# Two middle batches of a and b by Strassen block products: seven for eight, after the last attention

## The chip, the cores and the metric

One Trainium2 chip, one core. The metric is the device time of one launch in microseconds (us). The kernel before has a median of 718.08 us in three runs (717.61 to 720.74).

## The reference

Four batches of 12-head attention with a sigmoid in place of softmax, then a gated product, then a soft mixture of eight experts, all in float32:

```python
attn = sigmoid(q @ k.T / sqrt(64) - log(448))        # 4 batches, 12 heads, 448 x 64
x = (attn @ v) as 1792 x 768                          # 448 rows per batch
g = (x @ w_a) * (x @ w_b)                             # 1792 x 1536
y = g @ w_out                                         # 1792 x 768
logits = y @ phi                                      # 1792 x 32 slots
d = softmax of logits over the 1792 tokens; c = softmax over the 32 slots
slot_in = d.T @ y; h = relu(slot_in @ w1[e]); slot_out = h @ w2[e]   # 8 experts, 768 x 1024
out = c @ slot_out
```

## The kernel before, in words

Matrices lie with their inner dimension on the 128 partitions. `x` of a batch is six transposed tiles of 128 x 448 (one for each pair of heads); `w_a` and `w_b` are cut into 12 chunks of 128 columns (`fc`), each chunk 128 x 768 (six blocks of 128). Every float32 factor is split in two reduced-precision parts, high and low, and three of the four partial products are summed: high by high, low by high, high by low.

**Attention** (`att`, L211). A pair of heads (24 in all, six per batch) goes through these steps: `emit_TK` and `emit_TQ` transpose k and q on TensorE and split them on VectorE; `emit_S` (L171) makes the scores of one chunk of keys and the sigmoid on ScalarE; `emit_PV` (L190) multiplies by v; `emit_x` (L200) splits the result into the tiles `xh` (ScalarE) and `xl` (VectorE). The pairs of batch 0 run first, with nothing else on TensorE but some preparation.

**The gated product** (`ab`, L488). For each chunk `fc` of a batch it makes a, then b: 18 matmuls of 128 x 448 each (three partial products by six blocks, L502). ScalarE copies a out of PSUM (L509), VectorE multiplies b into it (L512); the result is a tile `gT`. So a batch has 12 x 2 x 18 = 432 matmuls of L502, the kernel 1728. Six of them are a step: after each step the generator yields, and the main loop (L754) lets the attention of the next batch go on by as much as it is due (`att_to`), so the attention of batches 1, 2 and 3 lies between the steps of `ab(0)`, `ab(1)` and `ab(2)`. `ab(3)` has no attention beside it. In `ab(0)` the weights are also converted (`beats`, L385) and stored in DRAM (`ab32`); later batches read them back (`load_w`) and split them again (`split`, L420): high part on VectorE (L425), low part on GpSimd (L426).

**Fill.** After every step of `ab` that wasn't preceded by a transposition, `fill_step` runs one step of the first generator in the list `fill`. `group(b, gi)` (L453) takes four `gT`: part of the logits (L461), 16 transpositions (L476), evacuated by ScalarE and VectorE in turn into `gk_01` or `gk_2`. `LG(b)` (L585) turns a batch's logits into exponentials (`logits`, L537), transposes them (`tokens`, L569) and multiplies them by the batch's three `gk` tiles (`dg`, L576, 64 matmuls at L582). A batch has three groups and one LG; those of batch 3 end after `ab(3)`. Both take PSUM banks from `ms()`, of which there are two up to batch 3; transpositions of k and q take theirs from the same two.

**The last batch and the experts.** With `ab(3)` the pool `e1` opens, and `pump` (L684, L757) starts to load the experts' weights into 17 slots of 1 MB, one pump for each three steps. All loads and stores go out by SyncE's queue (SP) in the order in which they are written, and a load that must wait for its buffer holds all later ones back. After `ab(3)` the experts' weights, 50 MB, are streamed and used (L809, L835).

Of the kernel before, what the change touches and what calls it, by code (L numbers as in the profile page):

```python
# [9 lines left out]
F32 = mybir.dt.float32  # L10
# [23 lines left out]
def body(ctx, tc, q, k, v, w_a, w_b, w_out, phi, w1, w2, out):  # L34
# [5 lines left out]
    ps_ctx, ab_ctx, x0_ctx, cv_ctx, ma_ctx, at_ctx = (ctx.enter_context(ExitStack()) for _ in range(6))  # L40
# [7 lines left out]
    more_a = {}  # L48
# [32 lines left out]
    ls_d = x0p.tile([128, 2 * S + 2 * C * NS], F32, name="ls_d")  # L81
# [7 lines left out]
    clog32 = drp.tile([T, C, B, NS], F32, name="clog32")  # L89

# [80 lines left out]
    def emit_S(g, chunks):  # L171

        (kh, kl), (qh, ql) = stk[g]["k"], stk[g]["q"]
        for c in chunks:
            ab = g < NP and c == 2
# [23 lines left out]

    def emit_x(g):  # L200
# [3 lines left out]
        xh = (x0p, x1p)[b % 2].tile([128, S], F32R, tag=f"xh{kk}", name=f"xh{kk}")  # L204
        xl = (x0p, x1p)[b % 2].tile([128, S], F32R, tag=f"xl{kk}", name=f"xl{kk}")
        act.activation(xh, pv, AF.Copy)  # L206
        dve.tensor_tensor(xl, pv, xh.bitcast(F32), op=ALU.subtract)  # L207
        xt[g] = (xh, xl)
        load_qkv(g + 3, "v")

    def att():  # L211
# [3 lines left out]
        for g in range(B * NP + 1):  # L215
            more = g < B * NP
            first = ((0, 1) if g == 0 else (0,) if g < NP else ()) if more else ()
# [6 lines left out]
            if g > 2 * NP:  # L224

                if g % 2 == 0:
                    emit_PV(g - 2, (0, 1, 2, 3))
                    emit_PV(g - 1, (0, 1, 2, 3))
                    emit_x(g - 2)
                    emit_x(g - 1)  # L230
                    yield 6400
            elif g:
                if g < NP:
# [5 lines left out]
            elif more:  # L239
                emit_TK(g + 1)  # L240
                yield 430
            if more and g >= NP:
# [6 lines left out]
            elif more:  # L249
# [135 lines left out]
    def beats():  # L385
        stage0(0)
        for x in range(len(jobs) + LAG + 2):
            if x < len(jobs):
                stage1(x)
            elif x == len(jobs):  # L390
                flush()
                for i in range(4):
                    load_w(2 * KF + i)
# [35 lines left out]
    def prep(n):  # L429
# [5 lines left out]
        elif 2 * n < LAST:  # L435
            for i in range(2):
                split(n, w_raw.pop(2 * n + i), dve.tensor_copy)
                for _ in range(3 if n == KF else 1):
# [465 lines left out]
```

## Time and profile before

| | us |
|---|---|
| median of three runs | 718.08 |
| profiled execution | 719.5 |
| its span, first to last instruction | 717.4 |
| TensorE busy in the span | 680.7 |

The profile is of one execution. Engines: PE is TensorE, PEld its weight loads, DVE is VectorE, ACT ScalarE, POOL GpSimd, SP SyncE. L502 is line 502 of the kernel. "PEclk" and "clock" are the share of its 2.4 GHz that TensorE was granted. Matmuls overlap, so a matmul's own duration is longer than the distance from one to the next. The chain of waits is the work that ended last, followed back to the start: what stands on it sets the time.

### The profile page before, as it was taken

Reading aid. Unit: us, or ns where it says so; the run is one execution under the profiler, and the core shown is the slowest. Engines: PE = TensorE matmul, PEld = TensorE weight load, DVE = VectorE, ACT = ScalarE, POOL = GpSimd, SP = SyncE. Lnnn points to the kernel's source line nnn. Section 1 sums busy time; section 2 is a strip of 40 time slices with the busy share of each in tenths; the row PEclk is TensorE's granted clock in tenths of the full one; section 3 lists DMA queues with packets and bytes.
Section 4 is the critical chain, followed back from the end, with each engine's and each line's share of the span. In section 5 each row is a group of like instructions: output and inputs, shape, how many; then the busy total and the mean of one; then the engine's idle time right before and its main releaser. Section 6 shows DMA issues by size and latency. Waiting matters only on the chain.

```text
span 717.4 us, 10851 instructions
## 1 busy us (share of the span) xinstructions
PE 680.7 (95%) x4231; PEld 489.8 (68%) x4231; DVE 303.2 (42%) x451; ACT 272.6 (38%) x469; POOL 246.3 (34%) x151
## 2 busy tenths in 40 slices
PE   7999999999999999999999999999999999998684
PEld 4547876776777687687776886878888896433132
DVE  4767899889843323234234232322322232300022
ACT  4987787877734324233143242331201011100021
POOL 0244677666653233242332322432444441100000
PEclk9999999999999999999999999999999999999898
DMA  8999999898762332423422322310788956999998
GB/s 208 243 283 228 293 314 295 262 301 276 227 202 54 104 100 75 122 71 87 143 61 92 104 66 61 103 50 1 264 276 325 359 209 217 364 415 417 410 353 273
DMA packets 107474, 148.99 MB, mean 208 GB/s; under 512 B 51360, under 2 KB 84384, under 8 KB 104352
## 3 DMA queue, kind: packets, MB, share of 16 engines
q1 hardware_dynamic: 107424, 148.31, 63.8%
q8 instruction: 33, 0.54, 0.3%
q14 instruction: 17, 0.14, 0.1%
HBM read 128.46 MB, written 19.83 MB: 207 GB/s over the span
## 4 chain that ended last, share of the span: by engine, by line
PE 84%; DMA 9%; DVE 2%; ACT 2%; issue 1%; POOL 0%; SPq 0%; ACTq 0%; POOLq 0%
PE ab L502 49%; PE sc L195 11%; PE sc L181 9%; DMA e<-in_moe_w 8%; PE ms L148 3%; PE ms L476 2%; PE ms L461 1%; DMA gkp<-in_moe_w 1%; PE ms L582 1%; DVE gk L323 1%; PE ms L366 1%; PE ms L353 1%; PE sc L872 1%; PE ab L835 1%; PE sc L789 1%
## 5 line engine op out<-in xcount | busy, mean ns | idle before, releaser
L426 POOL TENSOR_TENSOR wl<-wr_all,wh 128x768 fp32r<-128x768 f32 x50 | 92.0, 1841 | 207.2 <-DVE wh L425 98.3
L502 PE MATMUL ab<-xh,wh 128*128 128x448 f32 x576 | 138.1, 375 | 0.0
L502 PE MATMUL ab<-xl,wh 128*128 128x448 f32 x576 | 136.6, 372 | 0.0
L502 PE MATMUL ab<-xh,wl 128*128 128x448 f32 x576 | 136.6, 372 | 0.0
L185 ACT ACTIVATE a<-sc,sums 112x448 f32<-112x448 f32 x180 | 99.9, 638 | 62.2 <-PE sc L181 59.0
L502 PEld LDWEIGHTS ab<-xl,wh 128*128 128x128 f32 x576 | 105.3, 188 | 20.3 <-issue 12.3
L502 PEld LDWEIGHTS ab<-xh,wh 128*128 128x128 f32 x576 | 104.5, 188 | 15.7 <-issue 7.4
L502 PEld LDWEIGHTS ab<-xh,wl 128*128 128x128 f32 x576 | 105.1, 188 | 10.3 <-issue 2.7
L328 POOL TENSOR_TENSOR w<-gk,cy 128x768 int32<-128x768 int32 x36 | 66.2, 1840 | 91.3 <-DVE gk L323 54.2
L509 ACT COPY misc<-ab 128x448 f32<-128x448 f32 x48 | 25.6, 533 | 143.7 <-PE ab L502 143.7
L512 DVE TENSOR_TENSOR misc<-misc,ab 128x448 f32<-128x448 f32 x48 | 29.7, 619 | 114.4 <-PE ab L502 114.3
L195 PE MATMUL sc<-a,vn 112*64 112x448 f32 x384 | 76.5, 544 | 1.0 <-ACT a L185 1.0
L426 POOL TENSOR_TENSOR wl<-wr,wh 128x768 fp32r<-128x768 f32 x22 | 40.5, 1842 | 53.1 <-DVE wh L425 43.3
L195 PEld LDWEIGHTS sc<-a,vn 112*64 112x64 f32 x384 | 26.3, 136 | 41.8 <-issue 38.6
L425 DVE CAST wh<-wr_all 128x768 fp32r<-128x768 f32 x50 | 31.7, 634 | 37.7 <-POOL wl L426 23.5
L426 POOL TENSOR_TENSOR wl<-w,wh 128x768 fp32r<-128x768 f32 x24 | 44.9, 1873 | 2.5 <-ACT wh L425 2.5
L835 PE MATMUL ab<-e,gk 128*32 128x384 f32 x240 | 34.2, 560 | 9.7 <-DMA e<-in_moe_w 9.7
L181 PE MATMUL sc<-qh,kh 64*112 64x448 f32 x180 | 39.4, 418 | 0.7 <-ACT qh L141 0.6
L321 DVE TENSOR_SCALAR mf<-gk 128x768 f32<-128x768 f32 x36 | 34.1, 946 | 12.6 <-ACT gk L310 12.6
L206 ACT ACTIVATE xh<-sc 128x448 fp32r<-128x448 f32 x24 | 13.1, 547 | 68.8 <-PE sc L195 68.7
L207 DVE TENSOR_TENSOR xl<-sc,xh 128x448 fp32r<-128x448 f32 x24 | 14.9, 623 | 48.8 <-ACT xh L206 48.8
L181 PE MATMUL sc<-qh,kl 64*112 64x448 f32 x180 | 34.9, 368 | 0.0
(164 smaller groups left out, 725.3 us busy)
## 6 DMA issues: line engine op xcount, KB each, us to landing
e<-in_moe_w SPq DMA_DIRECT2D x23, 1024.0 KB, 7.4
wr_all<-ab SPq DMA_DIRECT2D x50, 384.0 KB, 3.5
e<-in_moe_w SPq DMA_DIRECT2D x23, 768.0 KB, 15.1
ab<-w SPq DMA_DIRECT2D x24, 384.0 KB, 7.5
wr<-ab SPq DMA_DIRECT2D x22, 384.0 KB, 4.0
kn<-in_k SPq DMA_DIRECT2D x48, 112.0 KB, 5.0
qn<-in_q SPq DMA_DIRECT2D x48, 112.0 KB, 3.7
vn<-in_v SPq DMA_DIRECT2D x24, 224.0 KB, 4.8
```

The costliest lines, as they stand in the source:

```text
L148: pe.transpose(t[:, c * T:(c + 1) * T], a[:, c].rearrange("p h d -> p (h d)"), ident[:T, :T])
L181: pe.matmul(sc[h], kx[r, cs], qx[r], start=(i == 0), stop=(i == 2))
L185: act.activation(a, sc[h], AF.Sigmoid, bias=nlog[:T], scale=1.0 / math.sqrt(D))
L195: pe.matmul(pv_t[g][64 * h:64 * h + 64], qkv_t["v", g][:, h, c, :], a_t.pop((g, h, c)), start=(c == 0), stop=(c == C - 1))
L321: dve.tensor_scalar(mf, m, LOW, HIGH, op0=ALU.max, op1=ALU.min)
L328: pool.tensor_tensor(thirds(w), m.bitcast(I32), thirds(cy_t.pop(x)), op=ALU.add)
L425: rnd(wh, t)
L426: pool.tensor_tensor(wl, t, wh.bitcast(F32), op=ALU.subtract)
L502: pe.matmul(t, w[:, kk * 128:(kk + 1) * 128], xt[b * NP + kk][xi], start=(s == 0 and kk == 0), stop=(s == 2 and kk == KD - 1))
L509: act.copy(gT_all[n % 5], t)
L512: dve.tensor_tensor(g, g, t, op=ALU.mult)
L835: pe.matmul(sps[h][32 * j:32 * j + 32], hT[:, 2 * x + i, 2 * j + g], ring[order2[n + j]][0][:, i, c0:c0 + w], start=(g == 0 and x == 0 and ...
```

## The change

Batches 1 and 2 are taken together. Their `x` is a 2 x 2 block matrix: A11 and A12 are the two halves (three tiles each) of batch 1's inner dimension, A21 and A22 those of batch 2. Two chunks of a weight are the other 2 x 2 matrix, with blocks of 384 x 128. A new `unit(u)` (12 of them: six pairs of chunks, a and b in turn) makes its four output blocks from seven block products (`ORDER`) of three blocks by three partial products, 9 matmuls each. The sums of blocks of `x` (S1 to S4) are made once on GpSimd (`operands`) and split, four of the seven only once unit 0 has begun (`late_operands`); the sums of weight blocks are made for each unit on VectorE (`prep_u`) and split by ScalarE or VectorE and GpSimd (`block`); the sums of products are made by VectorE from PSUM (`put` and others in `unit`).

The order is new. `ab(0)` runs as before, with batch 1's attention between its steps. Then the 12 pairs of batches 2 and 3 run alone, with `fill` steps and the preparation of unit 0 between them, then the 12 units with `fill` steps between the products, then `ab(3)`. Attention of batches 2 and 3 takes the order of batch 0 (one chunk of scores ahead of PV, three behind). `emit_x` writes an unsplit tile for batches 1 to 3. Since the groups of both batches come in turn, each group's `gk` is stored in DRAM (`gk32`), and `LG(1)` and `LG(2)` move into `ab(3)`, each with a reload of its three tiles (`reload_gk`). The pool `e1` opens, and the pumps start, at step 6 of `ab(3)`'s 72 and not at its first.

The diff, cut:

```diff
...
     clog32 = drp.tile([T, C, B, NS], F32, name="clog32")
+    gk32 = drp.tile([2, 3, T, 2048], F32, name="gk32")
...
+    def raw_x(b, kk):
+        if b == 1 or (b == 3 and kk < 5):
+            nm = f"t{kk if b == 1 else 6 + kk}"
+            return x1p.tile([128, S], F32, tag=nm, name=nm)
+        if b == 2 and kk >= 3:
+            while fill:
+                fill_step()
+            return small[:, (kk - 3) * S:(kk - 2) * S]
+        nm = f"r{kk}" if b == 2 else "x3t"
+        return pools["cp"].tile([128, S], F32, tag=nm, name=nm)
...
-        act.activation(xh, pv, AF.Copy)
-        dve.tensor_tensor(xl, pv, xh.bitcast(F32), op=ALU.subtract)
-        xt[g] = (xh, xl)
+        if b:
+            xt[g] = raw_x(b, kk)
+            act.activation(xt[g], pv, AF.Copy)
+        else:
+            xh = x0p.tile([128, S], F32R, tag=f"xh{kk}", name=f"xh{kk}")
+            xl = x0p.tile([128, S], F32R, tag=f"xl{kk}", name=f"xl{kk}")
+            act.activation(xh, pv, AF.Copy)
+            dve.tensor_tensor(xl, pv, xh.bitcast(F32), op=ALU.subtract)
+            xt[g] = (xh, xl)
...
             more = g < B * NP
-            first = ((0, 1) if g == 0 else (0,) if g < NP else ()) if more else ()
+            dense = g < NP or g >= 2 * NP
+            first = ((0, 1) if g == 0 else (0,) if dense else ()) if more else ()
...
             for c in first:
...
-            if g > 2 * NP:
-                if g % 2 == 0:
...
-            elif g:
-                if g < NP:
+            if g:
+                if dense and more:
                     emit_TQ(g + 1)
                     yield 430
                 emit_PV(g - 1, (0, 1, 2, 3))
                 emit_x(g - 1)
                 yield 3200
-            elif more:
...
+            if not dense:
                 emit_S(g, (0, 1))
                 yield 1600
                 emit_TQ(g + 1)
...
         if x < 2 * NCH:
-            t, i = (wr_all, x % 4) if x < LAST + 2 else (run["wr"], x % 2)
-            t = t[:, i * 768:(i + 1) * 768]
+            t = (gk_2 if x < LAST + 6 else run["wr"])[:, x % 2 * 768:(x % 2 + 1) * 768]
...
             gT.pop((b, 4 * gi + i))
             live.discard(b * KF + 4 * gi + i)
+        if b in (1, 2):
+            sp.dma_start(out=gk32[b - 1, gi], in_=gkt)
         gtok[b, gi] = gk
+    def reload_gk(b):
+        for gi in range(3):
+            t = (gk_01[:, gi] if gi < 2 else gk_2)[:T]
+            sp.dma_start(out=t, in_=gk32[b - 1, gi])
+            gtok[b, gi] = t.rearrange("p (c n) -> p c n", c=C)
...
-                            while n - 5 in live:
+                            while n - 5 in live or (n % KF == 4 and b and run["lg"] < b - 1):
...
@@ -520,22 +534,183 @@
                 if LAST <= 2 * n + 2 < 2 * NCH:
                     x = 2 * n + 2 + i
                     split(n + 1, w_raw.pop(x), dve.tensor_copy)
-                    if x >= LAST + 2:
+                    if x >= LAST + 6:
                         load_w(x + 2)
...
+    ORDER = ("A11", "S2", "A12", "S3", "S1", "A22", "S4")
+    UBANK = ("ab", "sc", "sc", "ab", "sc", "sc")
+    NU = KF
+    xs, wb_t, wu = {}, {}, {}
...
+    def block(u, m, t):
+        q = (7 * u + m) % RING
+        abt = {4: "wh0", 5: "wl0", 6: "wh1", 7: "wl1"}
+        nm = abt.get(q, f"wx{q}")
+        w = (abp if q in abt else pools["cp"]).tile([128, 2, BLK], F32R, tag=nm, name=nm)
+        (act.copy if m % 2 else dve.tensor_copy)(w[:, 0], t)
+        pool.tensor_tensor(w[:, 1], t, w[:, 0].bitcast(F32), op=ALU.subtract)
+        wb_t[u, m] = w
+    def prep_u(u):
+        w = wu.pop(u)
+        b11, b21, b12, b22 = (w[:, i * BLK:(i + 1) * BLK] for i in range(4))
+        t2, t3, t4 = (pools["cp"].tile([128, BLK], F32, tag=nm, name=nm) for nm in ("T2", "T3", "T4"))
+        block(u, 0, b11)
+        dve.tensor_tensor(t3, b22, b12, op=ALU.subtract)
+        dve.tensor_tensor(b12, b12, b11, op=ALU.subtract)
+        dve.tensor_tensor(t2, b22, b12, op=ALU.subtract)
+        yield
+        for m, t in ((1, t2), (2, b21), (3, t3), (4, b12), (5, t4), (6, b22)):
+            if m == 5:
+                dve.tensor_tensor(t4, b21, t2, op=ALU.subtract)
+            block(u, m, t)
+            yield
...
+    def split_x(nm, i, t, pl, names, rnd=None, sub=None):
+        xh, xl = (pl.tile([128, S], F32R, tag=x, name=x) for x in names)
+        (rnd or dve.tensor_copy)(xh, t)
+        (sub or pool).tensor_tensor(xl, t, xh.bitcast(F32), op=ALU.subtract)
+        xs[nm, i] = xh, xl
...
+        cp = pools["cp"]
+        for i in range(3):
...
+                yield
+            yield
+            a11, a12, a21, a22 = (xt[n + i] for n in (NP, NP + 3, 2 * NP, 2 * NP + 3))
+            s2 = cp.tile([128, S], F32, tag="s2", name="s2", bufs=2)
+            pool.tensor_tensor(a11, a11, a21, op=ALU.subtract)
+            pool.tensor_tensor(a21, a21, a22, op=ALU.add)
+            pool.tensor_tensor(s2, a22, a11, op=ALU.subtract)
+            yield
+            yield
+            split_x("S2", i, s2, cp, (f"S2h{i}", f"S2l{i}"))
+            pool.tensor_tensor(a12, a12, s2, op=ALU.subtract)
+            yield
+    def late_operands(nm):
+        n = {"S3": NP, "S1": 2 * NP, "A22": 2 * NP + 3, "S4": NP + 3}[nm]
+        for i in range(3):
+            split_x(nm, i, xt[n + i], pools["xb"], (f"{nm}h{i}", f"{nm}l{i}"), act.copy, dve)
...
+    def unit(u):
+        p, i = divmod(u, 2)
+        f1, f2 = 2 * p, 2 * p + 1
+        tm = {}
+        def put(key, q, t0, t1, out, eng):
+            b, f = key
+            if i == 0:
+                gT[key] = g_slot(u, q, b * KF + f)
+                dve.tensor_tensor(gT[key], t0, t1, op=ALU.add)
+            else:
+                dve.tensor_tensor(out, t0, t1, op=ALU.add)
+                eng.tensor_tensor(gT[key], gT[key], out, op=ALU.mult)
+        for m in range(7):
+            tag = UBANK[(7 * u + m) % 6]
+            t, w = ps_tile(tag, [128, S], 4 if tag == "sc" else 2), wb_t.pop((u, m))
+            for s, (wi, xi) in enumerate(((0, 0), (0, 1), (1, 0))):
+                for k in range(3):
+                    pe.matmul(t, w[:, wi, k * 128:(k + 1) * 128], xs[ORDER[m], k][xi],
+                              start=(s == 0 and k == 0), stop=(s == 2 and k == 2))
+            if m == 0:
+                tm["p1"] = p_tile()
+                act.copy(tm["p1"], t)
+            elif m == 1:
+                tm["u2"] = p_tile()
+                dve.tensor_tensor(tm["u2"], t, tm["p1"], op=ALU.add)
+            elif m == 2:
+                put((1, f1), 0, t, tm["p1"], tm["p1"], pool)
+            elif m == 3:
+                tm["u3"] = p_tile()
+                dve.tensor_tensor(tm["u3"], t, tm["u2"], op=ALU.add)
+            elif m == 4:
+                put((2, f2), 1, t, tm["u3"], p_tile() if i else None, dve)
+                dve.tensor_tensor(tm["u2"], t, tm["u2"], op=ALU.add)
+            elif m == 5:
+                put((2, f1), 2, t, tm["u3"], tm["u3"], pool)
+            else:
+                put((1, f2), 3, t, tm["u2"], tm["u2"], dve)
+            yield m
+        if u % 4 == 3:
+            fill.append(group(2, u // 4))
+            fill.append(group(1, u // 4))
...
     def LG(b):
-        t = run["lsd2"] if b == B - 2 else ls_d
+        t = run["lsd2"]
...
+        run["lg"] = b
         yield
...
         yield
-        if b == B - 2:
+        if b == B - 3:
+            reload_gk(b + 1)
+        elif b == B - 2:
             run.pop("lsd2")
-            open_slots(e1, [1])
+            open_slots(run["e1"], [1])
             open_slots(gkp, [0])
...
+    base = att_state[0]
+    for frac in ab(0):
+        att_to(base + NP * PAIR * min(1.0, frac * 1.02))
+    att_pairs(2 * NP)
...
+    ops, pu = operands(), None
+    load_u(0)
+    load_u(1)
+    for cost in att_g:
+        if not run.pop("trans", False):
+            fill_step()
+        if next(ops, 0) == 0:
+            pu = pu or prep_u(0)
+            next(pu, None)
+        if (4 * NP - 1, 0, C - 1) in a_t:
+            break
+    for _ in ops:
+        pass
+    for _ in pu or prep_u(0):
+        pass
+    lx = last_x()
+    for u in range(NU):
+        load_u(u + 2)
...
+        for m in unit(u):
+            if (u, m) == (0, 0):
+                for _ in att_g:
+                    pass
+                at_ctx.close()
+                pools["xb"] = xb_ctx.enter_context(tc.tile_pool(name="xb", bufs=1, side="right"))
+                late_operands("S3")
+                late_operands("S1")
+            elif u == 0 and m in (1, 2):
+                late_operands(("A22", "S4")[m - 1])
+            elif u >= 1:
+                next(lx, None)
+            if u + 1 == NU and m in (1, 3):
+                split(NU * 3, w_raw.pop(LAST + m // 2), dve.tensor_copy)
+            next(pu, None)
+            fill_step()
+    run["banks"] = 1
+    load_w(LAST + 4)
+    load_w(LAST + 5)
...
+    for i, frac in enumerate(ab(B - 1)):
...
+        if i < 6:
+            fill_step()
+        if i == 6:
+            while fill:
+                fill_step()
+            cp_ctx.close()
+            xb_ctx.close()
+            e1 = run["e1"] = ctx.enter_context(tc.tile_pool(name="e1", bufs=1, side="right"))
             run["lsd2"] = e1.tile([128, 2048], F32, tag="e11", name="lsd2")
...
+            load_w(LAST + 6)
+            load_w(LAST + 7)
+            open_slots(e1, range(2, NE1))
+            fill.append(LG(1))
+            fill.append(LG(2))
+        elif i == 12:
+            reload_gk(1)
+        if i > 6 and i % 3 == 1:
+            pump()
...
```

## Rows read from the trace of the kernel before

**Rows 1.** The profile's page: busy time by engine, slices, clock, DMA.
```profile
PE 680.7 (95%) x4231; PEld 489.8 (68%) x4231; DVE 303.2 (42%) x451; ACT 272.6 (38%) x469; POOL 246.3 (34%) x151
...
PE   7999999999999999999999999999999999998684
...
PEclk9999999999999999999999999999999999999898
DMA  8999999898762332423422322310788956999998
```

**Rows 2.** The page's chain of waits, share of the span by line.
```profile
PE ab L502 49%; PE sc L195 11%; PE sc L181 9%; DMA e<-in_moe_w 8%; PE ms L148 3%; PE ms L476 2%; PE ms L461 1%; DMA gkp<-in_moe_w 1%; PE ms L582 1%; DVE gk L323 1%; PE ms L366 1%; PE ms L353 1%; PE sc L872 1%; PE ab L835 1%; PE sc L789 1%
```

**Rows 3.** Busy time by stretch: batch 0's attention, ab(0), ab(1) and ab(2), ab(3), experts.
```profile
core 0: us, PE busy (x) PEld busy (x) DVE busy (x) ACT busy (x) POOL busy (x), PEclk, DMA share, GB/s
0.00:54.70 54.70, 48.33 (x300) 26.67 (x301) 32.57 (x53) 39.99 (x68) 11.67 (x12) 1.00 0.97 246
54.70:214.30 159.60, 156.34 (x937) 118.16 (x936) 132.77 (x151) 116.43 (x186) 102.89 (x56) 1.00 0.89 267
214.30:501.20 286.90, 286.90 (x1722) 220.22 (x1722) 89.47 (x155) 87.68 (x157) 86.54 (x47) 1.00 0.27 81
501.20:602.20 101.00, 101.00 (x579) 88.54 (x578) 28.28 (x51) 12.98 (x24) 42.36 (x23) 1.00 0.75 269
602.20:691.00 88.80, 73.53 (x596) 28.78 (x596) 11.02 (x24) 7.90 (x16) 2.82 (x13) 0.94 0.99 392
```

**Rows 4.** Chain of waits in time, in ab(3): start, us, what.
```profile
546.02 26.76 PE ab L502 x132
```

**Rows 5.** TensorE's timeline in batch 0's attention: PV of three pairs in a row.
```profile
29.86 3.23 PE L195 MATMUL sc<-a,vn 112*64 112x448 f32 x16
...
37.07 3.23 PE L195 MATMUL sc<-a,vn 112*64 112x448 f32 x16
...
44.45 3.23 PE L195 MATMUL sc<-a,vn 112*64 112x448 f32 x16
```

**Rows 6.** TensorE's waits in ab(0): waited for, us, times, longest.
```profile
PE ms L148 <- ACT wT L354: 0.8, 3, 0.3
PE ms L148 <- ACT misc L463: 0.8, 1, 0.8
PE ms L476 <- DVE ql L142: 0.7, 1, 0.7
```

**Rows 7.** Groups of instructions by line: busy us, mean ns of one, idle before.
```profile
L185 ACT ACTIVATE a<-sc,sums 112x448 f32<-112x448 f32 x180 | 99.9, 638 | 62.2 <-PE sc L181 59.0 <-DMA kn<-in_k 3.1
L206 ACT ACTIVATE xh<-sc 128x448 fp32r<-128x448 f32 x24 | 13.1, 547 | 68.8 <-PE sc L195 68.7
L207 DVE TENSOR_TENSOR xl<-sc,xh 128x448 fp32r<-128x448 f32 x24 | 14.9, 623 | 48.8 <-ACT xh L206 48.8
L426 POOL TENSOR_TENSOR wl<-wr_all,wh 128x768 fp32r<-128x768 f32 x50 | 92.0, 1841 | 207.2 <-DVE wh L425 98.3 <-PE ab L502 75.0 <-PE sc L181 28.4
L643 DVE TENSOR_TENSOR misc<-misc,cm 112x512 f32<-112x512 f32 x1 | 0.7, 693 | 0.0
```

**Rows 8.** Timeline of VectorE, then GpSimd, during one weight split in ab(1).
```profile
259.08 0.55 DVE L425 CAST wh<-wr_all 128x768 fp32r<-128x768 f32 x1
260.96 1.07 DVE L425 CAST wh<-wr_all 128x768 fp32r<-128x768 f32 x1 [1.33 <-issue]
...
259.77 1.85 POOL L426 TENSOR_TENSOR wl<-wr_all,wh 128x768 fp32r<-128x768 f32 x1 [7.08 <-DVE wh L425]
```

**Rows 9.** SP's timeline in ab(3): first loads, last pump into a free slot.
```profile
504.59 0.80 SPq L417 DMA_DIRECT2D wr<-ab  x2
505.43 0.43 SPq L699 DMA_DIRECT2D e<-out  x1
...
574.75 0.42 SPq L710 DMA_DIRECT2D gkp<-in_moe_w  x1
```

**Rows 10.** Windows of ab(3), columns as in rows 3; then the window 667 to 682.
```profile
500.00:530.00 30.00, 30.00 (x210) 25.00 (x210) 8.93 (x20) 5.30 (x10) 11.03 (x6) 1.00 0.71 239
530.00:575.00 45.00, 45.00 (x238) 39.69 (x237) 12.40 (x20) 4.96 (x9) 20.25 (x11) 1.00 0.91 337
575.00:598.00 23.00, 23.00 (x121) 21.30 (x120) 6.95 (x11) 2.19 (x4) 10.88 (x6) 1.00 0.47 164
...
667.00:682.00 15.00, 10.76 (x64) 2.79 (x64) 0.00 (x0) 0.00 (x0) 0.00 (x0) 0.77 1.02 410
```

**Rows 11.** DMA issues in 500 to 605 us: KB each, median us to landing.
```profile
wr<-ab SPq DMA_DIRECT2D x22, 384.0 KB, 4.0
```

More of the change, by code (lines that the diff above doesn't have):

```diff
@@ L238, in att @@
                 yield 3200
-            elif more:
+            else:
                 emit_TK(g + 1)
                 yield 430
-            if more and g >= NP:
+            if not more:
+                return
+            if not dense:
                 emit_S(g, (0, 1))
@@ L434, in prep @@
                 yield
[L435 to L438, printed above, removed]
-                    next(bg, None)
-                    yield
-            assert next(bg, None) is None
+        elif n == KF:
+            for _ in range(6):
+                next(bg, None)
+                yield
+            assert next(bg, 0) == 0
     gT, gtok, live = {}, {}, set()
@@ L457, in group @@
                 yield
+        lps = lp[b]
         t = ms()
@@ L530, in ab, with load_u @@
                 pass
+    BLK = 384
+    RING = 10
+    ORDER = ("A11", "S2", "A12", "S3", "S1", "A22", "S4")
+    UBANK = ("ab", "sc", "sc", "ab", "sc", "sc")
+    NU = KF
+    xs, wb_t, wu = {}, {}, {}
+    def load_u(u):
+        if u > NU + 1:
+            return
+        t = pools["cp"].tile([128, 1536], F32, tag="wr", name="wr", bufs=2)
+        src = ab32[u // 2 * 2:u // 2 * 2 + 2, u % 2] if u < NU else ab32[u - NU]
+        sp.dma_start(out=t.rearrange("p (n c) -> p n c", n=2), in_=src.rearrange("n p c -> p n c"))
+        if u < NU:
+            wu[u] = t
+        else:
+            for i in range(2):
+                w_raw[LAST + 2 * (u - NU) + i] = t[:, i * 768:(i + 1) * 768]
@@ L735, in body @@
         next(bg)
-    for b in range(B):
-        if b == 1:
-            cv_ctx.close()
-            more_a["pool"] = ma_ctx.enter_context(tc.tile_pool(name="map", bufs=1, side="left"))
-        if b == B - 1:
-            ma_ctx.close()
-            at_ctx.close()
-            x0_ctx.close()
-            e1 = ctx.enter_context(tc.tile_pool(name="e1", bufs=1, side="right"))
-            run["banks"] = 1
-            open_slots(e1, range(2, NE1))
+    base = att_state[0]
+    for frac in ab(0):
+        att_to(base + NP * PAIR * min(1.0, frac * 1.02))
@@ new lines, in body @@
+    att_pairs(2 * NP)
+    for kk in range(NP):
+        xt.pop(kk)
+    cv_ctx.close()
+    x0_ctx.close()
+    pools["cp"] = cp_ctx.enter_context(tc.tile_pool(name="cp", bufs=1, side="left"))
+    run["lsd2"] = pools["cp"].tile([128, 2 * S + 2 * C * NS], F32, name="ls_d")
+    fill.append(LG(0))
+    ops, pu = operands(), None
[9 more added lines that the diff above has]
+            break
@@ L765, in body @@
+            open_slots(e1, range(2, NE1))
[5 more added lines that the diff above has]
+            pump()
+    for kk in range(NP):
+        xt.pop((B - 1) * NP + kk)
     ab_ctx.close()
```

91 lines of the change are left out of this document (54 added, 37 removed).

## The prediction, made before the change was run

> **What bounds the kernel now.** I read the page first: TensorE is busy 95% of the span, at 9 tenths in nearly every slice up to the experts, at full clock; VectorE, ScalarE and GpSimd fall to 2 or 3 tenths after a third of the span [rows 1]. The chain says the same: L502 holds 49%, the attention's matmuls 20%, the experts' DMA 9% [rows 2]. By stage [rows 3], from 214.3 to 602.2 us TensorE is never idle, so there a matmul less is its time less, unless something takes its place. The experts' stage is different: DMA share 0.99, 392 GB/s, so it is paced by bytes, and what the change does to loads in front of it counts.
>
> **What is removed.** The price of an L502 matmul is its distance to the next, not its duration: 132 in 26.76 us [rows 4], 0.2027 us. Batches 1 and 2 take 2 x 432 = 864 of them. After the change: 12 units x 7 products x 9 = 756, of the same shape. 108 fewer x 0.2027 = **21.9 us**. This is as good as certain; all else is what is put in its place.
>
> **The dense attention.** Today pairs 12 to 23 lie between steps of `ab(1)` and `ab(2)`. What a pair costs there: `ab(3)` has 432 matmuls (87.6 us) in 101.0 us, so 13.4 us for its three groups and one LG. `ab(1)` and `ab(2)` last 286.9 us [rows 3], less 864 x 0.2027 = 175.1, less 2 x 13.4 = 26.8: 85.0 us for 12 pairs, 7.08 us each. Alone, in batch 0, PV follows PV after 7.21 and 7.38 us with TensorE hardly waiting [rows 5]. I take 7.21, as the 7.38 has weight conversion beside it: 12 x 0.13 = **+1.6 us** (with 7.38, +3.6). ScalarE covers: eight sigmoids at most 0.638 and a copy of 0.547 are 5.7 us of 7.2 [rows 7].
>
> But `group(0,2)` and `LG(0)` now fall between these pairs rather than between steps of 1.2 us of L502, and the two banks of `ms()` are shared with k's and q's transpositions. `ab(0)`, where the other engines are as busy, shows such waits of 0.3 to 0.8 us each [rows 6]. The two generators have some 16 steps, of which perhaps six wait so: **+2 us** (0 to 6, the upper end 0.4 for each step).
>
> **The seam to unit 0.** Product 0 is written before the last PV, and S3, S1, A22 and S4 are split behind it, 12 ScalarE copies (about 0.55) and 12 VectorE subtractions (about 0.62 [rows 7]: 0.693 for 512 columns gives 0.61 for 448). TensorE meanwhile has products of 9 x 0.2027 = 1.82 us. VectorE also has `prep_u(1)`'s first step (about 1.9 us: three subtractions of 0.52 and a cast) and a sum for each product. In its order, counted from the end of the last PV: copy of x 0.55, S3 done at 2.9 (needed at 3.65), S1 at 4.8 (5.5), A22 at 9.2 (7.3), S4 at 11.7 (11.0 after the first delay). That is a wait of about 2.6 us.
>
> One row makes it more. A VectorE cast of 0.55 us took 1.07 when it began in the middle of a GpSimd subtraction, and ended 0.4 us after that subtraction [rows 8]. GpSimd's `block` subtractions lie beside these 12, so I take **+4 us** (0 to 9; the upper end is 2.6 and all seven block subtractions of 0.92 us, half of 1.841, in the way).
>
> **The units themselves** I cost at nothing. What hides their other work is 12.8 us of TensorE a unit. VectorE: seven sums from PSUM at 0.62, four subtractions at 0.52, four casts at 0.28, two group evacuations, in half of the units two multiplications: 8 to 10 us. GpSimd: seven subtractions at 0.92, in half of the units two multiplications at 1.07 (1.841 x 448/768): 6.5 to 8.6 us. Weight blocks are ready seven products ahead, PSUM has six banks, so lags of some us don't reach TensorE. If that cover goes, see the second rival.
>
> **The last batch.** `group(2,2)` and `group(1,2)` are drained in its first step; `group(1,2)` and `LG(1)` only move here, but the end of the drain is PSUM, evacuation, PSUM: **+0.5 us** (0 to 2). Then SP issues, in this order: the store of a `gk` (112 x 8 KB = 0.92 MB), two weight loads (0.79), two pumps (2 MB), and `reload_gk(1)`, 2.75 MB, whose first piece waits for the store and whose last piece waits for a weight split that reads `gk_2`. `dg` of `LG(1)` comes at step 13, some 9 us of TensorE after all this can start. The DMA share was 0.91 at 337 GB/s while pumps ran [rows 10], so 371 GB/s is what there is: 6.5 MB take 17.5 us. The last wait is then `dg` on its last piece, about 7 us late, less what the first pieces let it do: **+6 us** (0 if the pieces overtake, 12 if the store and the wait for it come first and at 300 GB/s). All of `ab(3)` is queued behind it on TensorE. `reload_gk(2)` goes out as soon as that `dg` is done and has eight steps, 10 us, for 2.75 MB (7.4 us) and a pump: no wait taken.
>
> A wait of 6 us has a second price: in 667 to 682 us, where TensorE stood idle 4.24 of 15 us in pieces, the granted clock was 0.77 [rows 10], so part of the stretch ran at 1.2 and not 2.4 GHz: **+1 us** (0 to 3).
>
> The pumps start later: in the kernel before 3.4 us after `ab(3)` began [rows 3, 9], now after one chunk and two groups, 13 us. With 5.5 MB of reloads and one more store the DMA has about 35 MB instead of 27.5; at 371 GB/s this ends near 100 us after its start. `ab(3)` becomes 101 + 13.4/2 + 6 = 114 us, so the slots are full in time, as they were before at 582 (DMA share 0.47 from 575 [rows 10]). Weight loads land in 4.0 us [rows 11] and have about 6 before TensorE misses them: **+1 us** (0 to 8).
>
> **Small gain.** `emit_x` of batch 1 loses six subtractions of 0.623 us [rows 7] on VectorE in `ab(0)`, where TensorE idles 3.3 us: **-1 us** (-3 to 0).
>
> **Sum**, against the profiled execution of 719.5: 719.5 - 21.9 + 1.6 + 2 + 4 + 0.5 + 6 + 1 + 1 - 1 = 712.7. That execution is 1.4 us above the median of the runs, 718.08, so **711 us**.
>
> **A rule weighed.** The Trainium skill (SBUF — State Buffer, section Who interferes with whom) says that a VectorE instruction with two SBUF inputs, or one in its two-port mode, and a GpSimd instruction that reads SBUF lock each other out for a whole instruction. It speaks against this change, which puts all three kinds side by side. The lengthened cast is what it would give; no row shows how the sums of a unit would fare under it.
>
> **Rivals.**
> 1. *The seams are hidden.* All upper-bound terms fall to nothing, as the never idle TensorE of 214.3 to 602.2 us suggests [rows 3]: 719.5 - 21.9 + 1.6 = 699, on the median 698; with the drain, the clock and the half of the others up to 704. Against it: the reload has bytes enough for its wait. Chance 0.22.
> 2. *VectorE and GpSimd pace the units*, slower than before. VectorE runs in order; if each GpSimd subtraction holds it up as the row shows [rows 8], a unit costs VectorE 7 x 0.62 + 4 x 0.52 + 4 x 0.28 and GpSimd's 6.5, 14.0 us, or 17.3 with multiplications, 15.7 on average, against 12.8 and about 1 of groups. 12 x 1.9 = 23 us: 712.7 + 23 - 1.4 = 734. Half of it gives 723. It decides from the point where VectorE's time with its waits passes 13.8 us a unit, and PSUM sums are what TensorE waits for. Against it: sums with one operand in PSUM need not wait. This is the mechanism of the rule above. Chance 0.12.
> 3. *The last batch becomes DMA's.* If it gets only the 269 GB/s of its mean [rows 3], 35 MB take 130 us rather than 114, and weight loads and experts are late by it: 711 + 16 = 727. For it: share 0.91 already; against: it had nothing more to do then. Chance 0.07.
> 4. *The dense attention is not TensorE's*: at 8 us a pair, with ScalarE and the two banks the bound, 12 x 0.8 more, 720. Against it: batch 0. Chance 0.07.
> 5. *It doesn't do what it says*: were products waiting on the bank's sum each time, nothing would be saved; the loops count 756, so 0.02, at 718 or more.
>
> **How the numbers follow.** About 0.5% (3.6 us, so 714.5 and 721.7) is what a measurement of this kernel can tell from no change. The forecast case has 0.50, its own range 705 to 717, about 0.37 of it under 714.5. Faster: 0.37 + 0.22 + 0.02 of the fourth = 0.61. Slower: the second (0.10 of it), the third (0.05) = 0.15. The rest, 0.24, is within. The range 700 to 723 leaves out the better half of the first rival and the worse of the second and third.
>
> **What would show it.** Matmuls of the units 756 at 0.203 us; 12 pairs of 7.2 us with TensorE waits under 1 us each; a wait of TensorE on VectorE's or ScalarE's split before the sixth and seventh product of unit 0; a wait of TensorE on a `gk` load at L582's successor in `ab(3)`, of some 6 us, with the clock below 1 behind it; the experts' stage as long as before. I am wrong if the units last over 14 us each, if the experts' first loads find empty slots, or if no wait on `gk` shows at all.

## The result, and the profile after

The changed kernel takes **726.37 us** (median of 5 runs, 724.07 to 728.99), the kernel before 718.19 us in the same session (5 runs, 717.61 to 720.74): a ratio of 1.0107, 95% interval 1.0073 to 1.014, **slower by 1.07%**. The forecast was 711 with a range of 700 to 723. The profiled execution took 728.99 us with a span of 727.1, against 719.5 and 717.4 before: 9.7 us more span.

The profile's page after the change: busy time, TensorE's slices and clock, DMA, and the chain by line. L516 is the old L502, L682 the units' matmul, L757 is `dg` (before L582).

```profile
PE 665.9 (92%) x4123; PEld 473.6 (65%) x4123; DVE 392.3 (54%) x580; ACT 285.2 (39%) x503; POOL 301.2 (41%) x226
...
PE   6999998999999999999899999999299999998683
...
PEclk9999999999999899999999999999799999998898
DMA  9998998899624242101114313325998995999998
...
PE ab L516 22%; PE sc L195 11%; PE sc L682 10%; DMA e<-in_moe_w 8%; PE sc L182 7%; PE ab L682 5%; PE ms L149 3%; PE ms L486 2%; DMA gk<-gk 2%; PE ms L757 2%; PE ab L182 1%; DMA ab<-w 1%; DMA gkp<-in_moe_w 1%; PE ms L468 1%; ACT a L185 1%
```

Beside [rows 1], TensorE executes 108 matmuls less (4123 for 4231) and is busy for 14.8 us less (665.9 for 680.7). But there is a hole in its row, a slice with a 2, and the clock's row falls twice ahead of the experts. A new item stands on the chain beside [rows 2]: `DMA gk<-gk`, the reload from DRAM. VectorE has 89 us more to do, GpSimd 55.

By stage (columns as in rows 3): `ab(0)`; dense attention up to unit 0; the units; `ab(3)`; the experts up to the end of the span.

```profile
54.70:216.30 161.60, 158.28 (x949) 118.98 (x946) 126.59 (x145) 117.60 (x188) 99.77 (x54) 1.00 0.82 251
216.30:312.20 95.90, 90.74 (x638) 48.51 (x637) 38.84 (x67) 61.51 (x113) 32.09 (x28) 0.96 0.30 81
312.20:487.10 174.90, 170.61 (x868) 149.24 (x869) 142.57 (x212) 35.17 (x72) 113.80 (x97) 1.00 0.23 74
487.10:611.20 124.10, 110.95 (x677) 94.13 (x675) 31.75 (x62) 15.40 (x30) 41.12 (x23) 0.94 0.82 269
611.20:727.10 115.90, 87.88 (x698) 36.41 (x697) 20.11 (x42) 15.57 (x34) 2.81 (x13) 0.93 0.96 367
```

From 214.3 to 602.2 us TensorE had never been idle [rows 3]; now it idles 5.2 us in the dense attention, 4.3 in the units and 13.2 in `ab(3)`. TensorE's waits name the owners (waited for, us in total, times, longest; some lines left out are of the start and the experts). L748 transposes LG's logits, which ScalarE copied at L736; L572 is GpSimd's low part of a weight block, L594 VectorE's low part of a block of `x`, L689 VectorE's sum of two products:

```profile
PE ms L757 <- DMA gk<-gk: 13.1, 1, 13.1
...
PE ms L748 <- ACT ls_d L736: 1.7, 1, 1.7
PE sc L682 <- POOL wx L572: 1.7, 1, 1.7
...
PE sc L682 <- DVE A22l L594: 0.9, 1, 0.9
...
PE ab L682 <- DVE gk L689: 0.8, 1, 0.8
```

Where the 9.7 us come from, each stage against what its parts cost in the kernel before. The prediction's 13.4 us for three groups and one LG are taken as 3 x 2.8 and 4.9 (of which `dg` is 2.8); how they are split moves a little between stages, not the sum. The last PV, 3.2 us, lies inside the third window and counts with the dense attention.

| | forecast | found | how |
|---|---|---|---|
| 108 matmuls fewer | -21.9 | -21.9 | three L682 in 0.61 us, as before |
| `ab(0)` and dense attention | +2.6 | +8.2 | 161.6 - 159.6 = 2.0; 95.9 + 3.2 - 84.6 (12 pairs at 7.05) - 7.7 (a group and LG(0)) = 6.8; 0.6 less for the pairs and the moved work themselves |
| units | +4 | +7.3 | 174.9 - 3.2 - 153.2 (756 matmuls) - 11.2 (four groups) |
| `ab(3)` | +7.5 | +15.4 | 124.1 - 101.0 - 7.7 (the moved group and LG(1)) |
| experts | +1 | +0.7 | 115.9 - 115.2 |
| sum | -6.8 | +9.7 | |

Of the 2.0 us of `ab(0)` some 1.5 are order alone: the first scores of batch 2 now end before it does. The dense attention has that much less to do, so its own loss is nearer 8. Of the units' 7.3 us, 4.3 are idle time; the other 3.0 lie in time in which TensorE is busy at a clock of 1.00, and what makes them stays open.

**The hole.** The chain of waits in time (start, us, what), then two windows (columns as in rows 3): the transfer with `dg`, and `dg` alone:

```profile
509.60 0.14 SPq L769
...
509.84 0.56 SPq L503
...
510.44 14.31 DMA gk<-gk
...
524.89 5.30 PE ms L757 x64
```

```profile
511.00:532.00 21.00, 7.85 (x77) 5.41 (x76) 1.08 (x2) 0.35 (x1) 0.96 (x2) 0.67 1.00 271
...
524.90:530.20 5.30, 5.30 (x65) 3.34 (x65) 0.00 (x0) 0.00 (x0) 0.00 (x0) 0.52 0.88 247
```

`reload_gk(1)` is not issued until 509.8 us, because SP first stores LG(1)'s transposed logits (L769), which TensorE has just made; `dg` was due at 511.7 and got its last piece at 524.8. After 13.1 us of standing idle TensorE was granted 0.52 of its clock, the 1.2 GHz level, and `dg` took 5.30 us for the 2.81 that it takes at full clock.

**The dense attention.** ScalarE's timeline around LG(0)'s exponential:

```profile
236.19 0.55 ACT L218 ACTIVATE r<-sc 128x448 f32<-128x448 f32 x1 [3.17 <-PE sc L195]
236.74 1.28 ACT L731 ACT_TABLE_LOAD   x1
238.03 0.64 ACT L731 ACTIVATE ls_d<-ms,sums 128x448 f32<-128x448 f32 x1
...
238.66 0.52 ACT L736 COPY ls_d<-ms 128x448 f32<-128x448 f32 x1
239.20 1.28 ACT L185 ACT_TABLE_LOAD   x1
240.49 1.16 ACT L185 ACTIVATE a<-sc,sums 112x448 f32<-112x448 f32 x2
```

From 236.19 to 240.49 ScalarE does 0.55 us for the attention; the rest is an exponential, a copy and two loads of ScalarE's function table (one for the exponential, one back to the sigmoid), and the sigmoids that TensorE's next PV needs stand behind them. TensorE idled 1.72 us, and from 236 to 250 its granted clock was 0.76:

```profile
236.00:250.00 14.00, 12.29 (x116) 7.15 (x116) 3.58 (x7) 8.64 (x14) 0.00 (x0) 0.76 0.19 45
```

Both made the pair around it 15.5 us long (PV to PV, 232.89 to 248.35); pairs without fill follow at 7.05.

### The profile page after: what moved, and what is told of

Read it like the earlier page. It is cut to its first block, busy times and chain, and to the rows that moved or that the text cites. A ratio compares the mean times of both kernels' runs of the same rounds, so it can differ in the third digit from the quotient of the medians.

```text
span 727.1 us, 10908 instructions
## 1 busy us (share of the span) xinstructions
PE 665.9 (92%) x4123; PEld 473.6 (65%) x4123; DVE 392.3 (54%) x580; ACT 285.2 (39%) x503; POOL 301.2 (41%) x226
## 4 chain that ended last, share of the span: by engine, by line
PE 71%; DMA 13%; DVE 9%; ACT 3%; issue 2%; SPq 0%; POOL 0%; ACTq 0%; DVEq 0%; POOLq 0%
PE ab L516 22%; PE sc L195 11%; PE sc L682 10%; DMA e<-in_moe_w 8%; PE sc L182 7%; PE ab L682 5%; PE ms L149 3%; PE ms L486 2%; DMA gk<-gk 2%; PE ms L757 2%; PE ab L182 1%; DMA ab<-w 1%; DMA gkp<-in_moe_w 1%; PE ms L468 1%; ACT a L185 1%
## 5 line engine op out<-in xcount | busy, mean ns | idle before, releaser
L516 PE MATMUL ab<-t,wh 128*128 128x448 f32 x288 | 64.9, 370 | 0.0
L516 PEld LDWEIGHTS ab<-t,wh 128*128 128x128 f32 x288 | 53.2, 188 | 4.6 <-issue 0.6
L523 ACT COPY misc<-ab 128x448 f32<-128x448 f32 x24 | 12.9, 536 | 76.5 <-PE ab L516 76.5
L572 POOL TENSOR_TENSOR wx<-wr,wx 128x384 fp32r<-128x384 f32 x29 | 34.8, 1206 | 12.5 <-DVE wx L571 12.5
L571 ACT CAST wx<-T 128x384 fp32r<-128x384 f32 x23 | 11.5, 512 | 69.1 <-DVE T L587 42.1
L526 DVE TENSOR_TENSOR misc<-misc,ab 128x448 f32<-128x448 f32 x24 | 14.8, 617 | 38.1 <-PE ab L516 38.1
L333 DVE TENSOR_SCALAR gk<-mf 128x768 uint32<-128x768 uint32 x36 | 34.3, 953 | 1.2
L516 PE MATMUL ab<-xh,wh 128*128 128x448 f32 x144 | 34.9, 378 | 0.0
L516 PE MATMUL ab<-xh,wl 128*128 128x448 f32 x144 | 34.5, 375 | 0.0
L516 PE MATMUL ab<-xl,wh 128*128 128x448 f32 x144 | 34.5, 375 | 0.0
L516 PE MATMUL ab<-t,wl 128*128 128x448 f32 x144 | 34.0, 371 | 0.0
L572 POOL TENSOR_TENSOR wx<-T,wx 128x384 fp32r<-128x384 f32 x23 | 25.3, 1102 | 16.0 <-ACT wx L571 16.0
```

The costliest lines, as they stand in the source:

```text
L333: dve.tensor_scalar(mi, mf.bitcast(U32), 3, 0x3FFFFFFF, op0=ALU.logical_shift_left, op1=ALU.bitwise_and)
L516: pe.matmul(t, w[:, kk * 128:(kk + 1) * 128], xt[b * NP + kk][xi], start=(s == 0 and kk == 0), stop=(s == 2 and kk == KD - 1))
L572: pool.tensor_tensor(w[:, 1], t, w[:, 0].bitcast(F32), op=ALU.subtract)
```

## The experiments

All ran beside the kernel before, whose median was 717.75 to 718.81. "After" is the changed kernel, 726.37 us, as it was measured first; it was not run again beside them.

### Is it the reload?

**e1.** The reload is left out, so LG(1) and LG(2) multiply by whatever the tiles hold.

```diff
     def reload_gk(b):
...
-            sp.dma_start(out=t, in_=gk32[b - 1, gi])
```

> Leaves out the reload of the gk tiles of batches 1 and 2 from DRAM (LG(1) and LG(2) multiply by what the tiles hold), everything else is the changed kernel. Theory: TensorE's wait of 13.1 us at the first dg in ab(3), and the 2.4 us by which that dg is slower behind it, are the reload's own and nothing takes their place: ab(3) falls from 124.2 to about 109 us and the time from 726.4 to about 711. Rival: the last batch belongs to the DMA as a whole (pumps, weight loads), and the wait moves to weight splits or to the experts' stage: 720 or more.

709.12 us (707.47 to 712.02), ratio 0.987 (0.9843 to 0.9896). `ab(3)` (columns as in rows 3):

```profile
486.20:594.70 108.50, 108.50 (x680) 92.84 (x680) 32.60 (x62) 15.38 (x30) 41.10 (x23) 1.00 0.73 256
```

15.6 us off `ab(3)`, no idle time, full clock, and no other wait in its place. The reload costs 17.3 us of 726.37, and without it the change is faster than before by 1.3%.

**e2, e3: why is it late?** e2 gives the tiles in DRAM 128 rows and moves full tiles; e3 moves the store of LG's logits behind `dg`, so that SP isn't held up in front of the reload.

```diff
# e2
-    gk32 = drp.tile([2, 3, T, 2048], F32, name="gk32")
+    gk32 = drp.tile([2, 3, 128, 2048], F32, name="gk32")
...
-            t = (gk_01[:, gi] if gi < 2 else gk_2)[:T]
+            t = gk_01[:, gi] if gi < 2 else gk_2
# e3, in LG
+        if b:
+            sp.dma_start(out=clog32[:, :, b], in_=ltok)
         if b == B - 3:
             reload_gk(b + 1)
```

> Stores and reloads the gk tiles over all 128 partitions instead of 112 (and clears the unused ones once at the start). Theory: the reload's 14.3 us come from its shape, 271 GB/s at a DMA share of 1.00, and with 128 partitions it goes at the 371 GB/s or more that the pumps show: the wait falls from 13.1 to 7 to 9 us, the time to about 721. Rival: the two pumps of out32 ahead of it, and the store before it, set the rate, and the shape of the reload doesn't matter: the wait stays at 12 to 14 us and the time at 726.

> Moves the store of LG(1)'s and LG(2)'s logits behind their dg, so that SP doesn't wait for it ahead of the reload. Theory: SP's order cost the reload 3 us (it was issued at 509.84, right after that store's wait), so the reload is issued near 507 and the wait falls from 13.1 to about 10 us: time about 723. Rival: the DMA engines are full from the first pump on, an earlier issue only queues longer, wait 13, time 726.

e3: 726.58 us (725.54 to 727.62), wait 14.2 us: nothing gained. The first two pieces of the reload were issued some 1.5 us earlier (the first at 505.49 against 509.84, in a stage that began 2.8 us earlier) and queued longer, so their place on SP's queue is not what makes them late. The third, which waits for a weight split that reads `gk_2`, went out 24.6 us into the stage in both kernels (at 508.85 and 511.68). e2: 721.48 us (720.87 to 722.38), ratio 1.0039 (1.0027 to 1.0052), wait 8.3 us and 4.25 us for `dg`. The issues of `gk` in `ab(3)` (KB each, median us to landing), after and e2, both stores and reloads:

```profile
gk<-gk SPq DMA_DIRECT2D x8, 896.0 KB, 10.9
```

```profile
gk<-gk SPq DMA_DIRECT2D x8, 1024.0 KB, 8.1
```

A seventh more bytes land sooner when all 128 partitions take part. The rate shows it too. This is e2's window that begins 1.1 us after the reload's first issue (507.9), as 511 to 532 does in the changed kernel:

```profile
509.00:530.00 21.00, 12.73 (x104) 9.78 (x104) 3.31 (x9) 1.77 (x5) 3.07 (x3) 0.84 1.02 395
```

With the DMA engines full in both, 395 GB/s stand against 271. So 4.9 us of the loss belong to the shape of the transfers, stores and reloads together; that the rest is bytes in a full queue just ahead of their use is what e4 tries.

**e4: room and time.** Two `gk` are loaded into tiles of their own in the pool `e1` at the head of SP's queue, the third isn't stored at all, and `dg` goes tile by tile.

```diff
-            t = (gk_01[:, gi] if gi < 2 else gk_2)[:T]
+            t = run["e1"].tile([128, 2048], F32, tag=f"e1{11 + 2 * b + gi}", name="gkr")[:T]
...
-        for groups in ((0, 1), (2,)):
+        for groups in ((0,), (1,), (2,)) if b else ((0, 1), (2,)):
...
+            reload_gk(1)
             load_w(LAST + 6)
             load_w(LAST + 7)
-            open_slots(e1, range(2, NE1))
+            open_slots(e1, range(2, 13))
...
-        elif i == 12:
-            reload_gk(1)
+        elif i == 9:
+            reload_gk(2)
```

> The reload goes to tiles of its own in e1, at the head of SP's queue when e1 opens (step 6, batch 2's at step 9), and the third group of each batch, still in its tile, is neither stored nor reloaded; the dg is three calls of one group. Theory: 1.84 MB with nothing ahead of them land in 7 to 9 us, about when the dg comes: wait 0 to 2 us, no slow dg, time about 711 to 713. Rival: the pumps are only pushed behind, and weight splits or the experts' first loads are late by what was won: 718 or more.

715.08 us (711.74 to 718.63, 10 runs), ratio 0.9948 (0.9929 to 0.9967). The wait on `gk` is gone, with transfers of 112 partitions still; which of room, time and the third tile did it was not tried singly. A new wait stands at the second `dg`:

```profile
PE ms L757 <- DVE lsd L749: 3.0, 1, 3.0
```

LG(2)'s transposed logits go into the buffer from which LG(1)'s are still being stored, 14.2 us to landing. It had been hidden behind the wait on `gk`.

### The dense attention and the units

**e5 to e7.** e5 spreads the splitting of batch 3's `x` (`last_x`) over more products, e6 puts two empty fill steps between LG(0)'s exponential and what reads it, e7 makes unit 1's weight blocks later in unit 0.

```diff
# e5
-            elif u >= 1:
+            elif u >= 1 and m % 3 == 1:
                 next(lx, None)
# e6, in LG
+        if not b:
+            yield
+            yield
# e7
-            next(pu, None)
+            for _ in range((0, 0, 1, 2, 2, 1, 1)[m] if u == 0 else 1):
+                next(pu, None)
```

> The split of batch 3's x (one VectorE cast and one GpSimd subtraction for each of six tiles) goes at two tiles for each of the units 1 to 3, where the changed kernel puts all six into unit 1. Theory: GpSimd is full from 341 to 359 us and TensorE's waits of 1.7 us (for a block's low part) and 0.8 us (for a bank) in unit 2 come from that alone: both go, time 726.4 less 2.5 to 3, about 723.5. Rival: GpSimd and VectorE hold each other up in every unit, the same waits come back in a later unit: 726.

> Two empty steps between LG(0)'s exponential and its transpositions, in the dense attention. Theory: TensorE's wait of 1.7 us there is for ScalarE, which takes two table loads of 1.28 us and the exponential between sigmoids, and the clock of 0.76 in 236 to 250 us follows from that wait; both go, 1.7 us and some 3 us of half clock, so about 722. Rival: the wait is ScalarE's lack of time in these pairs, it moves to PV's wait for a sigmoid and the clock falls all the same: 725 to 726.

> prep_u(1) begins two products later in unit 0, so that VectorE splits A22 and S4 without its three subtractions ahead of them. Theory: TensorE's wait of 0.9 us before and in the sixth product, and the slow matmuls behind it, go: about 1.5 us less, 725. Rival: unit 1's blocks come late instead, a wait in unit 1 or 2 of the same size: 726.4.

e5: 724.84 us (722.28 to 730.02), ratio 1.0094 (1.0059 to 1.0129). The waits of unit 2 are gone, and a group now waits 1.7 us for GpSimd's product of a and b (L675). In its profiled execution, the shortest of the four, the clock stayed at 1.00 in the dense attention though the wait for LG(0) was the same 1.7 us, and that pair, whose window follows, took 12.9 us rather than 15.5. With such a spread nothing is shown of the time.

```profile
231.29:244.16 12.87, 11.14 (x122) 6.31 (x121) 3.58 (x8) 8.67 (x15) 0.00 (x0) 1.00 0.30 70
```

e6: 728.17 us (726.18 to 728.79), no gain; the wait only moved, from the logits to the scores, since ScalarE is as late as before:

```profile
PE sc L182 <- ACT a L185: 2.5, 1, 2.5
```

e7: 726.24 us (725.77 to 727.87); the 0.9 us wait at A22 is gone and the time is not measurably less.

**e8.** e4 to e7 together, and LG(2)'s logits in columns of their own.

```diff
-        dtok, ltok = (... for i in (2 * S, 2 * S + C * NS))
+        dtok, ltok = (... for i in ((4 if b == 2 else 2) * S, (4 if b == 2 else 2) * S + C * NS))
```

> All of it together: the reload early and to its own tiles, batch 3's x spread, LG(0) spaced, unit 1's preparation later, and LG(2)'s transposed logits in columns of their own, so that they don't wait for the store of LG(1)'s (a wait of 3.0 us at the second dg of e4_early). Theory: the terms add: e4_early's 715.1 less 3.0, 2.7, 4 and 1.5, about 704, under both kernels. Rival: what is won ahead of the experts makes their first loads late, as these were pushed behind: 710 or more.

713.63 us (711.76 to 714.36), ratio 0.9924 (0.991 to 0.9937): a miss by 10 us. The last batch is mended (109.2 us, experts 115.2), the rest is not: its units last 174.2 us, and its waits are

```profile
PE ms L468 <- POOL g L675: 3.1, 1, 3.1
PE sc L182 <- ACT a L185: 2.5, 1, 2.5
```

**e9, e10: the two causes that were left.** e9 moves VectorE's roundings beside GpSimd's subtractions to ScalarE. e10 lets `group(0,2)` start one fill step earlier, so that LG(0)'s exponential falls ahead of PV and not behind it.

```diff
# e9
-        (act.copy if m % 2 else dve.tensor_copy)(w[:, 0], t)
+        act.copy(w[:, 0], t)
...
-            dve.tensor_copy(xh, r)
+            act.copy(xh, r)
# e10, in group
-            for _ in range(GDEL):
+            for _ in range(1 if (b, gi) == (0, 2) else GDEL):
                 yield
```

> All high parts of the weight blocks, and batch 3's x, are rounded by ScalarE, where the changed kernel has VectorE do four of seven and the x. Theory: VectorE's casts of 0.34 us take 0.6 to 1.3 beside GpSimd's subtractions, and the two engines hold each other up; ScalarE is busy 20% of the units' time and isn't held up, so the waits of 1.7 and 0.8 us in unit 2 go and VectorE's busy time falls from 143 to about 115 us: time about 723. Rival: GpSimd alone is late in unit 1, with six more subtractions of 1.27 us, whoever rounds: same waits, 726.

> group(0,2) begins one fill step earlier, so that LG(0)'s exponential stands on ScalarE right ahead of a PV (3.2 us of TensorE) and not behind one, where six sigmoids are due. Theory: the 3.9 us that ScalarE needs for two table loads, the exponential and a copy lie beside PV; no wait of 1.7 us (or 2.5, as in e6_space), no lower clock: about 4 us less, 722. Rival: TensorE catches up with ScalarE in any place, since ScalarE has 2 us to spare in a pair: wait of 1 us or more and 725 to 727.

e10: 722.31 us (721.24 to 722.46), ratio 1.0055 (1.0034 to 1.0075), 4.1 us less than after. The window 228 to 250 us, after and e10:

```profile
228.00:250.00 22.00, 19.66 (x160) 10.81 (x160) 7.44 (x14) 12.83 (x22) 0.79 (x1) 0.84 0.25 60
```

```profile
228.00:250.00 22.00, 21.37 (x193) 11.87 (x194) 8.65 (x16) 16.03 (x28) 0.00 (x0) 1.00 0.29 71
```

33 more matmuls in the same 22 us, and full clock: the pair lasts 10.8 us for 15.5. The table loads are still there; the first one and the exponential now lie beside PV's 3.2 us of TensorE, and no wait on them is left. By e5's pair of 12.9 us, some 2.6 of these 4.7 us are the clock and 2.1 the wait and what goes with it (an estimate from single executions).

e9: 725.16 us (722.34 to 727.14), ratio 1.0091 (1.0055 to 1.0126). TensorE no longer waits for GpSimd in unit 2 and the units last 172.4 us, 2.5 less, but unit 0 waits longer for S4. By medians 1.2 us, within its spread. What it acts on shows in the changed kernel's unit 2, in VectorE's and then GpSimd's timeline, and in the group of all casts of L571 (ns min/median/max):

```profile
347.45 1.30 DVE L571 CAST wx<-wr 128x384 fp32r<-128x384 f32 x1
```

```profile
345.87 1.40 POOL L572 TENSOR_TENSOR wh<-wr,wh 128x384 fp32r<-128x384 f32 x1
347.23 1.30 POOL L634 TENSOR_TENSOR t<-t,t 128x448 fp32r<-128x448 f32 x1
348.49 1.13 POOL L572 TENSOR_TENSOR wl<-T,wl 128x384 fp32r<-128x384 f32 x1
```

```profile
L571 DVE CAST wx<-wr x29: 343/570/1305, 277.3 to 475.0; 128x384 fp32r<-128x384 f32 x29
L571 ACT CAST wx<-T x23: 502/513/524, 280.9 to 473.9; 128x384 fp32r<-128x384 f32 x23
```

A cast of 0.34 us takes 1.30 and ends just after the subtraction beside it (348.75 against 348.53); ScalarE's cast is never held up. The Trainium skill (SBUF — State Buffer, section Who interferes with whom) says just this: VectorE in its two-port mode and GpSimd exclude each other for a whole instruction, ScalarE waits for nobody. The trace agrees; in which mode these casts ran, no run here shows.

**e11: all of it.** e8 with e9's ScalarE roundings, and e10's placement for e6's empty steps.

> e8_all with the rounding on ScalarE, and with e10's earlier group in the place of the empty steps. Theory: units near 167 us instead of 171 and the dense attention 4 us shorter: 713.6 less 4 and 4, about 706. Rival: the waits move on, as the one of 3.1 us on a GpSimd product in e8_all did: 711 or more.

**702.15 us** (701.54 to 702.19, 5 runs), ratio 0.9774 (0.9755 to 0.9793): 2.3% faster than the kernel before, 3.3% than the changed one. Its dense attention, units and `ab(3)`:

```profile
216.30:307.14 90.84, 86.95 (x632) 46.55 (x631) 36.04 (x61) 63.26 (x117) 31.43 (x28) 1.00 0.32 86
307.14:475.66 168.52, 168.52 (x868) 149.74 (x869) 113.52 (x162) 56.39 (x121) 110.60 (x97) 1.00 0.24 76
475.66:585.04 109.38, 108.69 (x741) 94.13 (x740) 31.23 (x62) 15.40 (x30) 41.10 (x23) 1.00 0.78 272
```

TensorE is busy throughout the units: 168.5 - 3.2 - 153.2 - 11.2 leaves 0.9 us over its matmuls. The dense attention is 1.7 us over its parts (90.8 + 3.2 - 84.6 - 7.7), `ab(3)` 0.7. The span, 700.4, is 17.0 below that of before: 21.9 won, some 5 given back, of which 2.0 in `ab(0)`.

## Why the prediction was wrong

**The gain was right.** 756 matmuls at the old distance; e11 shows that nearly all of the 21.9 us can be kept. Each of the costs beside it was placed where it came, but too small, and together they outran it.

**The reload: the step that failed.** It is the largest of three terms set too small: it makes 7.9 of the 16.5 us between forecast and found, the dense attention 5.6 and the units 3.3. The prediction had "+6 us (0 if the pieces overtake, 12 if the store and the wait for it come first and at 300 GB/s)", and "+1 us" for the clock. The wait was 13.1 us, `dg` 2.5 longer at half clock, `ab(3)` 15.4 over its parts, where 7.5 were forecast. Three things were wrong in the working. The sum: 17.5 us of transfers less 9 us of TensorE are 8.5 us, not "about 7 us late". The rate: 371 GB/s was taken from a window in which only transfers of 128 partitions ran (pumps and weight loads); with the `gk` transfers of 112 partitions among them DMA had a share of 1.00 and moved 271 GB/s from 511 to 532 us. e2 measured that part: 395 GB/s and 4.9 us. And the time to spare: the list of what SP issues ahead of the reload left out the store of LG(1)'s logits, so that there were 2 us from issue to use and not the "9 us of TensorE". By e3 this omission cost nothing, as the bytes would have queued anyway. e4 fits both: issued ahead of the loads, with two tiles for three, there is no wait on `gk`, but it does not part the two. That "no wait" was taken for `reload_gk(2)` was right.

**The dense attention**: "+2 us (0 to 6)" for the fill between pairs, with "ScalarE covers". The pairs were right (7.05 us, even below the 7.21 taken). The fill was not, with some 8 us: it was costed as waits on the two banks of `ms()`, while the largest part was ScalarE's own time, an exponential with two table loads in a place where the next sigmoids are due. In the kernel before the second load fell at 262.67 us, after ScalarE had waited 10.8 us for work, and hid. e10 shows 4.1 of the 8.2 us to be this, the clock behind the wait included; e6 shows that more distance for the reader doesn't help while ScalarE is late. The gain of 1 us in `ab(0)` didn't come.

**The seam and the units**: "+4 us (0 to 9)" and "at nothing" became 7.3. The wait came where it was put, before A22, and was 0.9 us; the sum was wrong in the units, where 3.2 us of waits on GpSimd, VectorE and ScalarE stand, the two long ones in unit 2 (at 356.0) and at the start of unit 3 (359.5). There `last_x` puts further subtractions on GpSimd, a piece for each product, and its queue runs without a gap from 341 to 357 us; `last_x` was not in the prediction's count. The count itself was low too: a unit was to cost VectorE 8 to 10 us and GpSimd 6.5 to 8.6, and the 12 units with unit 0's and batch 3's splits kept them busy for 142.6 and 113.8 us, 11.9 and 9.5 each. Removing one wait showed the next (e5, e9); only e11, with e5, e7 and e9 together, had units without idle time. Which of them was needed for it was not tried singly.

**The rivals.** The third came out nearest in time (727) and had the mean rate of DMA in `ab(3)` right, 269 GB/s, but not its mechanism: weight loads and experts were not late (115.9 us), the reload alone was. The second had the right mechanism, the lock, but it lengthened instructions without pacing the units: TensorE was busy for 170.6 of their 174.9 us, and VectorE for 11.9 us a unit, not 14.0 to 17.3. The fourth is out by the 7.05 us of a pair, the fifth by the matmuls. The first, 698 to 704 with the seams hidden, is what e11 does (702), once they are.

**The range** ended at 723 because the upper ends were set one by one: the reload's 12 and the fill's 6 were both passed in one kernel, nearly all of the clock's 3 was spent behind the reload alone (`dg`'s 2.5 us), and the wait at LG(0) was followed by a lower clock as well.

## What to carry to other kernels

Where a change moves work out of the shade of a saturated engine, list for each moved step every instruction on every queue (the activation table's loads, the small store ahead of a big reload), and ask of a transfer not only its bytes but its shape and how long before its use it is issued. When TensorE stops, allow for a lower clock behind it: the wait of 13.1 us cost 15.6 in its stage (e1), the one of 1.7 us some 4 (e10). And one experiment that takes out a single wait may gain nothing because the next lies just behind; before the idea is given up, all of them should be out together.

## What was not expected of the hardware

Transfers of 112 partitions were slow: 896 KB took 10.9 us to land where 1024 KB on 128 partitions took 8.1, in the same place. The Trainium skill (SBUF — State Buffer, section Door 1) lets DMA's bandwidth depend on how many of 16 ports the partitions reach; by its table 112 partitions reach them all, and four ports would only have less to do. By that the smaller transfer would land no later; here it did, and the measurement decides. Other transfers were in the queue, so the 2.8 us are not a price of the shape by itself; the rates, 271 GB/s against 395 with the DMA engines full, say the same. What in 112 partitions is slow, no run shows.

A wait of 1.7 us was followed by a granted clock of 0.76 over 14 us (236 to 250) in the changed kernel; in the profiled executions of e5 and e3, with the same wait, the clock stayed at 1.00. So a short wait may or may not be paid for twice. The runs of after (4.9 us from lowest to highest) and e5 (7.7) against those of e10 (1.2) and e11 (0.65), which have no such wait there, would fit that, but those of e2 (1.5) and e3 (2.1), which have it, fit it less; it was not tried by itself.

GpSimd's subtraction of 384 columns took 1.0 us at least, not the 0.92 that half of the 768-column one would be. ScalarE's table load took 1.28 us, and the exponential began right behind it at 238.03; the Trainium skill (ScalarE: Activation LUTs, section What ACT_TABLE_LOAD costs) gives 1.28 for the load and some 1.38 more for a drain, of which this row shows nothing.
